# A delta rule in chunks of 64 tokens on quarter-array tiles, with 32-row blocks inverted on VectorE, instead of chunks of 128 inverted on TensorE

## The chip, the cores and the metric

One core of a Trainium2 chip runs the whole program. The metric is device time in microseconds of one launch; 1698.51 us is the median of three runs (1691.02 to 1699.28).

## The reference

Two blocks follow each other, all in float32. The first is a delta rule over 4 x 8 sequences (batch, head) of 768 tokens with 48 features. Each token reads its output and then updates a 48 x 48 state:

```
k_n = k / (norm(k) + 1e-6)
for t in range(S):
    y[t]  = q[t] @ state                 # the state before this token
    v_old = k_n[t] @ state
    state = state + beta[t] * outer(k_n[t], v[t] - v_old)
```

The outputs, 3072 tokens of 8 x 48 = 384 features, go to a router: cosine similarity to 8 expert embeddings over tau, softmax, and the first largest takes the token. The expert computes gate * relu(x @ w1[e]) @ w2[e] with 1024 hidden features.

## The kernel before

**Chunks.** A chunk is 128 tokens of one batch entry with its 8 heads; tokens lie on the partitions. With kb = beta k, a chunk needs z from (I + A) z = v - k S, where A is the strictly lower part of k kb^T; then y = q S + lower(q kb^T) z and S += kb^T z. There are 6 chunks a sequence and 4 batch entries.

**The functions.** `load` (L149) brings k, q and v of a chunk in pieces of 192 bytes, on SyncE's DMA queue. `prep` (L185 to L196) makes the norms, k over its norm and kb on GpSimd, heads padded to 64 columns. `front` transposes k, q and kb two heads at a time (L207, copied out at L208), multiplies them (L215) and masks the products (L220 on VectorE, L222 and L223 on ScalarE and GpSimd); L228 and L229 make the first W, the transposed inverses of the diagonal blocks of two rows.

**The inversion.** `invert` takes two batch entries at once, four groups of four heads. Six levels double the block from 2 to 128 rows. Each level transposes W (L240, copied at L242), multiplies by A (L248, masked at L251) and multiplies again (L257, added at L260), always whole 128 x 128 matrices, one head each.

**The steps.** `back` does what needs the state: k S (L268), R = v - k S (L271), z = W^T R (L276, copied at L279), q S (L284) plus the masked product times z (L287), the state's update (L299, L303), and the transposes and logits for the router (L307, L312, L313). `route` (L321 to L362) ranks each token within its expert, writes the outputs to DRAM (L343) and scatters token numbers into the experts' lists (L362).

**The experts.** 19 tiles of 256 tokens, each with one expert's weights. Per tile: gathered tokens are transposed (L447, L448), multiplied by w1 (L454, L456) and w2 (L460), scaled by the gate (L463) and scattered to the output (L464).

**What orders the work.** The code is written stage by stage, but a planner puts the instructions of each engine into a fixed order when the program is built: an instruction can be placed ahead of earlier code when its inputs and buffers are planned to be free. The engines then run their orders and wait on semaphores. PSUM's eight banks are shared out by two tags: `big` with five buffers, `seq` with three.

Of the kernel before, what the change touches and what calls it, by code (L numbers as in the profile page):

```python
# [15 lines left out]
C = 128  # tokens in a chunk of the delta rule  # L16
T = 256  # tokens in a tile of the experts
LEVELS = (2, 4, 8, 16, 32, 64)
# [3 lines left out]
def kernel(  # L22
# [30 lines left out]
    NMAP = E * N + NT * T  # L53

# [3 lines left out]
    idmap = tc.dram_tile([NMAP, 1], I32, name="idmap")  # L58

    def big(shape):  # L60
        return ps.tile(shape, F32, name="big", tag="big", bufs=5)

    def seq(shape):
        return ps.tile(shape, F32, name="seq", tag="seq", bufs=3)

# [5 lines left out]
    half = cpool.tile([128, B, H], F32, name="half")  # L71
    nc.vector.memset(half, 0.5)
    mask_su = cpool.tile([128, 1, 128], F32, name="mask_su")
    nc.gpsimd.memset(mask_su, 1.0)
    nc.gpsimd.affine_select(out=mask_su, in_=mask_su, compare_op=ALU.is_ge, fill=0.0, base=-1,
                            pattern=[[0, 1], [1, 128]], channel_multiplier=-1)
# [8 lines left out]
    tokid = cpool.tile([128, NC, B], I32, name="tokid")  # L85
    nc.gpsimd.iota(tokid, pattern=[[C, NC], [S, B]], base=0, channel_multiplier=1)
# [4 lines left out]
    nc.sync.dma_start(idmap.rearrange("(p n) o -> p (n o)", p=128), none)  # L91
    zrow = cpool.tile([1, Dm + 1], F32, name="zrow")
    nc.vector.memset(zrow, 0.0)
    nc.sync.dma_start(x_dram[N:N + 1, :], zrow)
# [5 lines left out]
    ac = att.enter_context(tc.tile_pool(name="ac", bufs=1))  # L100
    io = att.enter_context(tc.tile_pool(name="io", bufs=2))
# [3 lines left out]
    xor_i = ac.tile([128, 128], I32, name="xor_i")  # L105
    row_i = ac.tile([128, 128], I32, name="row_i")
    nc.gpsimd.iota(xor_i, pattern=[[1, 128]], base=0, channel_multiplier=0)
    nc.gpsimd.iota(row_i, pattern=[[0, 128]], base=0, channel_multiplier=1)
    nc.vector.tensor_tensor(xor_i, xor_i, row_i, op=ALU.bitwise_xor)
    xor_f = ac.tile([128, 128], F32, name="xor_f")  # L110
    nc.vector.tensor_copy(xor_f, xor_i)
    nmask1 = ac.tile([128, 1, 128], F32, name="nmask1")
    nc.vector.scalar_tensor_tensor(out=nmask1[:, 0, :], in0=xor_f, scalar=1.0, in1=mask_su[:, 0, :],
                                   op0=ALU.is_equal, op1=ALU.mult)
    nc.vector.tensor_scalar_mul(nmask1, nmask1, -1.0)
# [251 lines left out]
    for c in range(NC):  # L367
        V4 = loaded[1]
        if c + 1 < NC:
            loaded = load(c + 1)  # L370
# [133 lines left out]
```

## Time and profile before

| What | Value |
|---|---|
| Median of three runs | 1698.51 us |
| Span of the profiled execution (first to last instruction; no other time is given for it) | 1703.2 us |
| Instructions | 23067 |
| Mean granted TensorE clock | 0.864 of 2.4 GHz |
| Matmuls / busy | 9723 / 1476.8 us |
| VectorE, ScalarE, GpSimd busy | 568.2, 318.2, 350.3 us |
| DMA pieces, bytes | 114233, 92.62 MB |

The profile is one execution on the chip. PE is the matmul side of TensorE and PEld its weight loads, which overlap; DVE is VectorE, ACT ScalarE, POOL GpSimd, SP SyncE. A `q` behind an engine's name means its instruction queue, which issues DMAs. L12 is line 12 of the kernel. In a group, the shapes are output and input; a mean is the time of one instruction, which for matmuls includes time in the pipeline, so the spacing of a group on the timeline tells more of the pace.

### The profile page before, as it was taken

Reading aid. Unit: us, or ns where it says so; the run is one execution under the profiler, and the core shown is the slowest. Engines: PE = TensorE matmul, PEld = TensorE weight load, DVE = VectorE, ACT = ScalarE, POOL = GpSimd, SP = SyncE. Lnnn points to the kernel's source line nnn. Section 1 sums busy time; section 2 is a strip of 40 time slices with the busy share of each in tenths; the row PEclk is TensorE's granted clock in tenths of the full one; section 3 lists DMA queues with packets and bytes.
Section 4 is the critical chain, followed back from the end, with each engine's and each line's share of the span. In section 5 each row is a group of like instructions: output and inputs, shape, how many; then the busy total and the mean of one; then the engine's idle time right before and its main releaser. Section 6 shows DMA issues by size and latency. Waiting matters only on the chain. (4 is left out here: it accounts for less than half of the span.)

```text
span 1703.2 us, 23067 instructions
## 1 busy us (share of the span) xinstructions
PE 1476.8 (87%) x9723; PEld 1318.2 (77%) x9723; DVE 568.2 (33%) x1015; ACT 318.2 (19%) x613; POOL 350.3 (21%) x330
## 2 busy tenths in 40 slices
PE   3698969989698997989889897989739999999997
PEld 2697959979597996979789796979737666677774
DVE  4542525344362543526343352625401111001010
ACT  2122222121222212122212212222100000111110
POOL 7703042020503004030310204020021111111110
PEclk9786959789697977969788896979769999999999
DMA  9100030001200010000100000000045554555540
GB/s 144 19 1 10 1 65 1 6 5 20 47 1 10 1 43 6 1 10 1 38 1 1 1 1 19 2 1 1 19 171 184 173 180 159 163 179 178 165 145 0
DMA packets 114233, 92.62 MB, mean 54 GB/s; under 512 B 81137, under 2 KB 103849, under 8 KB 114130
## 3 DMA queue, kind: packets, MB, share of 16 engines
q1 hardware_dynamic: 108290, 78.80, 16.3%
q0 software_dynamic: 5632, 12.24, 2.6%
q8 instruction: 76, 1.25, 0.3%
q14 instruction: 27, 0.22, 0.0%
q10 hardware_dynamic: 208, 0.11, 0.0%
HBM read 81.55 MB, written 12.33 MB: 55 GB/s over the span
## 5 line engine op out<-in xcount | busy, mean ns | idle before, releaser
L251 DVE TENSOR_TENSOR Pm<-big,nmask 128x512 f32<-128x512 f32 x288 | 198.1, 691 | 308.8 <-PE big L248 308.8
L248 PE MATMUL big<-Ti,LM 128*128 128x128 f32 x2304 | 290.7, 288 | 0.0
L248 PEld LDWEIGHTS big<-Ti,LM 128*128 128x128 f32 x2304 | 285.9, 206 | 0.0
L257 PE MATMUL big<-W,Pm 128*128 128x128 f32 x2304 | 271.0, 276 | 9.1 <-DVE Pm L251 9.1
L257 PEld LDWEIGHTS big<-W,Pm 128*128 128x128 f32 x2304 | 264.8, 193 | 9.5 <-DVE Pm L251 9.5
L242 ACT ACTIVATE Ti<-big 128x512 f32<-128x512 f32 x288 | 152.7, 601 | 563.9 <-PE big L240 563.9
L240 PE MATMUL big<-ident,W 128*128 128x128 f32 x1152 | 157.8, 288 | 105.3 <-POOL W L229 105.3
L240 PEld LDWEIGHTS big<-ident,W 128*128 128x128 f32 x1152 | 134.8, 148 | 120.0 <-POOL W L229 116.7
L454 PE MATMUL big<-xTm,w 128*128 128x256 f32 x912 | 204.4, 384 | 18.4 <-DVE xTm L448 18.4
L260 DVE TENSOR_TENSOR W<-big,W 128x512 f32<-128x512 f32 x288 | 199.0, 691 | 57.6 <-PE big L257 57.5
L454 PEld LDWEIGHTS big<-xTm,w 128*128 128x128 f32 x912 | 173.5, 192 | 46.3 <-DVE xTm L448 23.0
L460 PE MATMUL seq<-w,hT 128*128 128x384 f32 x608 | 199.2, 486 | 0.0
L460 PEld LDWEIGHTS seq<-w,hT 128*128 128x128 f32 x608 | 115.5, 190 | 76.5
L463 DVE TENSOR_SCALAR y<-seq,xg 128x384 f32<-128x384 f32 x38 | 23.5, 618 | 390.5 <-PE seq L460 390.5
L196 POOL TENSOR_TENSOR KK<-KK,betaT 128x384 f32<-128x384 f32 x24 | 19.8, 830 | 600.4 <-PE seq L299 600.4
L456 ACT ACTIVATE hT<-big 128x512 f32<-128x512 f32 x76 | 45.4, 597 | 407.5 <-PE big L454 407.5
L464 POOL DMA_INDIRECT out_dram<-y,ids x38 | 38.3, 1008 | 239.5 <-DVE y L463 239.5
L215 PE MATMUL big<-KT 48*128 48x256 f32 x384 | 75.1, 511 | 10.0 <-ACT KT L208 10.0
L215 PEld LDWEIGHTS big<-KT 48*128 48x128 f32 x384 | 53.1, 248 | 22.0 <-ACT KT L208 14.8
L287 PE MATMUL seq<-Z,LM 128*128 128x48 f32 x384 | 66.4, 343 | 2.3 <-ACT Z L279 2.3
L287 PEld LDWEIGHTS seq<-Z,LM 128*128 128x128 f32 x384 | 65.2, 264 | 2.9 <-ACT Z L279 2.9
L436 POOL DMA_INDIRECT xg<-x_dram,ids x38 | 37.1, 977 | 130.6 <-DMA ids<-idmap 119.7
(131 smaller groups left out, 1076.9 us busy)
## 6 DMA issues: line engine op xcount, KB each, us to landing
w<-in_moe_w_dram SPq DMA_DIRECT2D x38, 1536.0 KB, 7.0
x_dram<-xc SPq DMA_DIRECT2D x6, 770.0 KB, 4.3
K<-in_k_dram SPq DMA_DIRECT2D x24, 192.0 KB, 4.1
V<-in_v_dram SPq DMA_DIRECT2D x24, 192.0 KB, 4.1
Qp<-in_q_dram SPq DMA_DIRECT2D x24, 192.0 KB, 2.9
xg<-x_dram,ids POOLq DMA_INDIRECT x38, 3.4
out_dram<-y,ids POOLq DMA_INDIRECT x38, 3.1
idmap<-tokid,slot_i POOLq DMA_INDIRECT x24, 4.1
```

The costliest lines, as they stand in the source:

```text
L215: nc.tensor.matmul(psG[:, i], lhsT=KT[pr, 2 * g + i, 2, :], rhs=KT[pr, 2 * g + i, 0:2, :], start=True, stop=True, skip_group_check=True)
L240: nc.tensor.transpose(psI[:, j, :], W[:, j, :], ident)
L242: nc.scalar.activation(Ti, psI, ACT.Copy)
L248: nc.tensor.matmul(psP[:, j, :], lhsT=AT[:, j, :], rhs=Ti[:, j, :], start=True, stop=True, skip_group_check=True)
L251: nc.vector.tensor_tensor(Pm, psP, nmask[s].broadcast_to([128, NP, 128]), op=ALU.mult)
L257: nc.tensor.matmul(psW[:, j, :], lhsT=Pm[:, j, :], rhs=W[:, j, :], start=True, stop=True, skip_group_check=True)
L260: nc.vector.tensor_tensor(Wn, psW, W, op=ALU.add)
L287: nc.tensor.matmul(psY[:, h, :], lhsT=LM[:, h % 2, h // 2, 1, :], rhs=Z[:, h, :], start=(c == 0 and h == 0), stop=True, skip_group_check=True)
L454: nc.tensor.matmul(psH[:, i, :], lhsT=w1[:, j, (f + i) * 128:(f + i + 1) * 128], rhs=xT[:, j, :], start=(j == 0), stop=(j == KC - 1))
L456: nc.scalar.activation(hT[:, f:f + 2, :], psH, ACT.Relu)
L460: nc.tensor.matmul(psO, lhsT=hT[:, f, t * 128:(t + 1) * 128], rhs=w2[:, f, :], start=(f == 0), stop=(f == NF - 1))
L464: nc.gpsimd.indirect_dma_start(out=out[:, :], out_offset=bass.IndirectOffsetOnAxis(ap=ids[:, t:t + 1], axis=0), in_=y, in_offset=None, bou ...
```

## The change

The chunk has 64 tokens, and two batch entries (g = 0, 1) are stacked on the partitions: tokens of the first on partitions 0 to 63, of the second on 64 to 127. With p the pair of entries, a superstep takes two chunks of both pairs, four tiles j; there are six supersteps. All products of the delta rule become matmuls on 64 x 64 tiles of the array (48 x 64 where the features are contracted), with the two halves written one after the other.

`front(s)` loads, normalizes, transposes k and q into KQ, multiplies k by k and q in one matmul per head and half (psG), and masks with beta folded into the mask (mb). `invert(s)` copies the 32 x 32 diagonal blocks of A through DRAM so that each of the 128 blocks (4 block rows by 32 heads) has one partition, inverts them there by forward substitution on VectorE (31 pairs of operations), copies the inverses back through DRAM, transposes them in blocks of 32 and makes the lower corner of each 64-row inverse with two products. `step` is the old `back` for a tile. The loop runs front and invert of superstep s + 1 ahead of the steps of s.

The sums of squares are taken tile by tile, k and q are loaded by half (24 transfers a superstep), and the outputs of a superstep are stored in four transfers instead of one per chunk. PSUM is shared out as `two` (three buffers of two banks) and `one` (two buffers of one bank), also in the experts. The constants for the old levels go. Initial transfers that don't belong to the loads move from SyncE's queue to ScalarE's.

```diff
-C = 128  # tokens in a chunk of the delta rule
-LEVELS = (2, 4, 8, 16, 32, 64)
+C = 64
+Q = 32
...
+    a_dram = tc.dram_tile([2, 4, J * H, Q, Q], F32, name="a_dram")
+    t_dram = tc.dram_tile([2, 4, J * H, Q, Q], F32, name="t_dram")
+    def two():
+        return ps.tile([128, 2, 512], F32, name="two", tag="two", bufs=3)
+    def one(shape):
+        return ps.tile(shape, F32, name="one", tag="one", bufs=2)
...
     def load(c):
+        Ks, Vs = [], []
+        for p in range(P2):
+            Kt = io.tile([128, H, D], F32, name="K", tag="K", bufs=4)
+            Vt = io.tile([128, H, D], F32, name="V", tag="V", bufs=8)
+            for dst, src in ((Kt, k), (Qs[(c * P2 + p) % len(Qs)][:, :, 0:D], q), (Vt, v)):
+                for g in range(2):
+                    nc.sync.dma_start(out=dst[64 * g:64 * g + 64],
+                                      in_=src[2 * p + g, :, c * C:(c + 1) * C, :].rearrange("h t d -> t h d"))
+            Ks.append(Kt)
+            Vs.append(Vt)
+        return Ks, Vs
+    def front(s):
+        data = [load(2 * s + i) for i in range(2)]
+        rn = wk.tile([128, J, H], F32, name="rn", tag="rn")
...
+        A = wk.tile([128, J, H, C], F32, name="A", tag="A")
+        kts, pts, kbs, vs = [], [], [], []
...
+            mb = wk.tile([128, 2, NP, C], F32, name="mb", tag="mb")
             for hh in range(2):
+                nc.gpsimd.tensor_tensor(mb[:, hh], later.broadcast_to([128, NP, C]),
+                                        bh.rearrange("p (a b) -> p b a", b=2)[:, hh].unsqueeze(2)
+                                        .broadcast_to([128, NP, C]), op=ALU.mult)
+            KQ = wk.tile([128, NP, 2, 2, C], F32, name="KQ", tag="KQ", bufs=8)
+            for i, src in enumerate((kn, qp)):
+                psT = one([128, NP, 2, C])
+                for hp in range(NP):
+                    nc.tensor.transpose(psT[:, hp].rearrange("p g t -> p (g t)"),
+                                        src[:, 2 * hp:2 * hp + 2, :].rearrange("p h d -> p (h d)"), ident)
+                nc.scalar.activation(KQ[:, :, :, i, :], psT, ACT.Copy)
+            psG = two()
+            for hp in range(NP):
+                for g in range(2):
+                    for hh in range(2):
+                        r = slice(64 * hh, 64 * hh + D)
+                        nc.tensor.matmul(psG[64 * g:64 * g + 64, hh, 128 * hp:128 * hp + 128],
+                                         lhsT=KQ[r, hp, g, 0, :], rhs=KQ[r, hp, g, :, :],
+                                         start=True, stop=True, skip_group_check=True)
+            pg = psG.rearrange("p a (b i t) -> p (a b) i t", i=2, t=C)
+            Pt = wk.tile([128, H, C], F32, name="P", tag="P", bufs=8)
+            mbf = mb.rearrange("p a b t -> p (a b) t")
+            nc.vector.tensor_tensor(A[:, j], pg[:, :, 0, :], mbf, op=ALU.mult)
+            nc.vector.tensor_tensor(Pt, pg[:, :, 1, :], mbf, op=ALU.mult)
...
+    def invert(s, A):
+        Bk = wk.tile([128, Q, Q], F32, name="Bk", tag="Bk", bufs=1)
+        for b in range(4):
+            nc.sync.dma_start(out=a_dram[s % 2, b].rearrange("h s t -> s h t"),
+                              in_=A[Q * b:Q * b + Q, :, :, Q * (b % 2):Q * (b % 2) + Q]
+                              .rearrange("s j h t -> s (j h) t"))
+        nc.sync.dma_start(out=Bk, in_=a_dram[s % 2].rearrange("b h s t -> (b h) s t"))
+        Tk = wk.tile([128, Q, Q], F32, name="Tk", tag="Tk", bufs=1)
+        nc.gpsimd.tensor_copy(Tk, eye)
+        for i in range(Q - 1):
+            sh = [128, Q - 1 - i, i + 1]
+            tmp = wk.tile([128, 256], F32, name="tmp", tag="tmp")
+            tv = tmp[:, 0:sh[1] * sh[2]].rearrange("p (a b) -> p a b", b=sh[2])
+            nc.vector.tensor_tensor(tv, Bk[:, i, i + 1:Q].unsqueeze(2).broadcast_to(sh),
+                                    Tk[:, i:i + 1, 0:i + 1].broadcast_to(sh), op=ALU.mult)
+            nc.vector.tensor_tensor(Tk[:, i + 1:Q, 0:i + 1], Tk[:, i + 1:Q, 0:i + 1], tv, op=ALU.subtract)
+        Td = wk.tile([128, J * H, Q], F32, name="Td", tag="Td", bufs=1)
+        nc.sync.dma_start(out=t_dram[s % 2].rearrange("b h s t -> (b h) s t"), in_=Tk)
+        for b in range(4):
+            nc.sync.dma_start(out=Td[Q * b:Q * b + Q], in_=t_dram[s % 2, b].rearrange("h s c -> s h c"))
+        Wd = wk.tile([128, J * H, Q], F32, name="Wd", tag="Wd", bufs=1)
+        nc.vector.transpose(Wd.rearrange("p h t -> p (h t)"), Td.rearrange("p h t -> p (h t)"))
+        Tz = wk.tile([128, J * H, Q], F32, name="Tz", tag="Tz", bufs=1)
+        nc.scalar.activation(Tz, Td, ACT.Copy, scale=first)
+        W = wk.tile([128, J * H, C], F32, name="W", tag="W")
+        nc.scalar.activation(W[:, :, 0:Q], Wd, ACT.Copy, scale=first)
+        for j in range(J):
+            psP = one([128, H, Q])
+            for h in range(H):
+                for g in range(2):
+                    r = slice(64 * g, 64 * g + 64)
+                    nc.tensor.matmul(psP[r, h, :], lhsT=A[r, j, h, :], rhs=Tz[r, j * H + h, :],
                                      start=True, stop=True, skip_group_check=True)
+            PI = PIs[j % len(PIs)]
+            nc.scalar.activation(PI[:, :, 0:Q], psP, ACT.Copy, scale=nsec)
+            psW = one([128, H, Q])
+            for h in range(H):
+                for g in range(2):
+                    r = slice(64 * g, 64 * g + 64)
+                    nc.tensor.matmul(psW[r, h, :], lhsT=PI[r, h, :], rhs=Wd[r, j * H + h, :],
                                      start=True, stop=True, skip_group_check=True)
+            nc.scalar.activation(W[:, j * H:(j + 1) * H, Q:C], psW, ACT.Copy)
+        return W
+    def step(s, j, KQ, Pt, kb, V, W, xc, ssx, lz):
+        c, p = 2 * s + j // P2, j % P2
+        Sp = St[p]
+        R = wk.tile([128, 2, NP, D], F32, name="R", tag="R")
+        Vv = V.rearrange("p (b a) d -> p a b d", a=2)
+        def heads(ps2):
+            return ps2[:, :, 0:NP * D].rearrange("p a (b d) -> p a b d", d=D)
+        psY = two()
+        yv = heads(psY)
         if c > 0:
+            psK = two()
+            kv = heads(psK)
+            for i, pv in ((0, kv), (1, yv)):
+                for hp in range(NP):
+                    for g in range(2):
+                        for hh in range(2):
+                            r = slice(64 * hh, 64 * hh + D)
+                            nc.tensor.matmul(pv[64 * g:64 * g + 64, hh, hp, :], lhsT=KQ[r, hp, g, i, :],
+                                             rhs=Sp[r, g, hp, :], start=(hp == 0), stop=True, skip_group_check=True)
+            nc.vector.tensor_tensor(R, Vv, kv, op=ALU.subtract)
+        else:
+            nc.vector.tensor_copy(R, Vv)
+        psZ = one([128, H, D])
+        Rf = R.rearrange("p a b d -> p (a b) d")
+        for h in range(H):
+            for g in range(2):
+                r = slice(64 * g, 64 * g + 64)
+                nc.tensor.matmul(psZ[r, h, :], lhsT=W[r, j * H + h, :], rhs=Rf[r, h, :],
                                  start=True, stop=True, skip_group_check=True)
         Z = wk.tile([128, H, D], F32, name="Z", tag="Z")
         nc.scalar.activation(Z, psZ, ACT.Copy)
+        if c < NC - 1:
+            psS = two()
+            sv = heads(psS)
+            for hp in range(NP):
+                for g in range(2):
+                    for hh in range(2):
+                        r = slice(64 * g, 64 * g + 64)
+                        nc.tensor.matmul(sv[64 * hh:64 * hh + 64, g, hp, :], lhsT=kb[r, 2 * hp + hh, :],
+                                         rhs=Z[r, hh * NP + hp, :], start=True, stop=True, skip_group_check=True)
+            nc.vector.tensor_tensor(Sp, Sp, sv, op=ALU.add)
+        for hp in range(NP):
+            for hh in range(2):
+                for g in range(2):
+                    r = slice(64 * g, 64 * g + 64)
+                    nc.tensor.matmul(yv[r, hh, hp, :], lhsT=Pt[r, hh * NP + hp, :], rhs=Z[r, hh * NP + hp, :],
+                                     start=(c == 0 and hp == 0), stop=True, skip_group_check=True)
+        xb = xc[:, j, 0:Dm]
+        nc.scalar.activation(xb.rearrange("p (b a d) -> p a b d", a=2, d=D), yv, ACT.Copy)
...
+    ahead = front(0)
+    W = invert(0, ahead[0])
+    for s in range(NS):
+        _, kts, pts, kbs, vs = ahead
+        xc = io.tile([128, J, Dm + 1], F32, name="xc", tag="xc")
+        ssx = wk.tile([128, J], F32, name="ssx", tag="ssx")
+        lz = wk.tile([128, J, E], F32, name="lz", tag="lz")
+        Wn = None
+        if s + 1 < NS:
+            ahead = front(s + 1)
+            Wn = invert(s + 1, ahead[0])
+        for j in range(J):
+            step(s, j, kts[j], pts[j], kbs[j], vs[j], W, xc, ssx, lz)
+        route(s, xc, ssx, lz)
+        W = Wn
...
-            psX = big([128, KC, 128])
+            psX = one([128, KC, 128])
...
-            psH = big([128, 2, T])
+            psH = two()
...
-            psO = seq([128, Dm])
+            psO = one([128, Dm])
```

## Rows read from the trace of the kernel before

**Rows 1.** The page: busy us, share of span, instructions by engine.
```profile
PE 1476.8 (87%) x9723; PEld 1318.2 (77%) x9723; DVE 568.2 (33%) x1015; ACT 318.2 (19%) x613; POOL 350.3 (21%) x330
```

**Rows 2.** Windows by stage: busy us (count) per engine, then clock, DMA share, GB/s.
```profile
50.00:1238.00 1188.00, 1045.24 (x8003) 1000.94 (x8002) 506.12 (x894) 262.57 (x520) 233.01 (x208) 0.82 0.05 12
1238.00:1276.00 38.00, 15.58 (x57) 12.61 (x58) 1.11 (x2) 2.39 (x4) 7.88 (x9) 0.61 0.52 187
1276.00:1703.00 427.00, 398.49 (x1578) 290.36 (x1576) 40.18 (x74) 43.00 (x72) 70.45 (x71) 0.99 0.48 153
```

**Rows 3.** Groups by line and shape: count, busy us, mean ns, idle before, TensorE.
```profile
L248 PE MATMUL big<-Ti,LM 128*128 128x128 f32 x2304 | 290.7, 288 | 0.0
...
L257 PE MATMUL big<-W,Pm 128*128 128x128 f32 x2304 | 271.0, 276 | 9.1 <-DVE Pm L251 9.1
...
L240 PE MATMUL big<-ident,W 128*128 128x128 f32 x1152 | 157.8, 288 | 105.3 <-POOL W L229 105.3
```

**Rows 4.** Timeline, one inversion level: start us, duration us, line, count.
```profile
287.83 3.74 PE L248 MATMUL big<-Ti,LM 128*128 128x128 f32 x32
...
296.72 3.74 PE L248 MATMUL big<-Ti,LM 128*128 128x128 f32 x32
```

**Rows 5.** Windows of ten us between two inversions: engines, then the granted clock.
```profile
215.00:225.00 10.00, 9.42 (x55) 9.08 (x55) 0.17 (x1) 1.45 (x4) 0.00 (x0) 0.50 0.46 79
```

**Rows 6.** Timeline, matmul groups outside the inversion, at both clock levels.
```profile
35.56 2.10 PE L215 MATMUL big<-KT 48*128 48x256 f32 x16 [0.69 <-ACT KT L208]
...
223.93 1.10 PE L299 MATMUL seq<-Z,KK 128*64 128x48 f32 x16
...
317.25 0.67 PE L299 MATMUL seq<-Z,KK 128*64 128x48 f32 x16
...
331.64 1.06 PE L207 MATMUL big<-ident,KK 128*128 128x128 f32 x4
```

**Rows 7.** Groups by line and shape, GpSimd and ScalarE.
```profile
L228 POOL TENSOR_TENSOR W<-LM,nmask 128x512 f32<-128x512 f32 x48 | 60.9, 1269 | 11.2 <-DVE LM L220 10.2
...
L196 POOL TENSOR_TENSOR KK<-KK,betaT 128x384 f32<-128x384 f32 x24 | 19.8, 830 | 600.4 <-PE seq L299 600.4
...
L279 ACT ACTIVATE Z<-seq 128x384 f32<-128x384 f32 x24 | 11.8, 491 | 168.5 <-PE seq L276 168.5
```

**Rows 8.** VectorE: two groups, then two dependent operations on the timeline.
```profile
L220 DVE TENSOR_TENSOR LM<-big,mask_su 128x512 f32<-128x512 f32 x48 | 33.2, 691 | 54.3 <-PE big L215 54.3
...
L271 DVE TENSOR_TENSOR R<-V,seq 128x384 f32<-128x384 f32 x20 | 11.1, 554 | 33.2 <-PE seq L268 33.2
...
234.67 0.17 DVE L354 TENSOR_TENSOR run<-run,rk 128x8 f32<-128x8 f32 x1
...
234.87 0.17 DVE L353 TENSOR_TENSOR rk<-rk,run 128x8 f32<-128x8 f32 x1
```

**Rows 9.** DMA: 10 to 30 us, 216 to 232 us, page's scatter.
```profile
q1 hardware_dynamic: 18002, 3.47, 119.3%
...
Qp<-in_q_dram SPq DMA_DIRECT2D x1, 192.0 KB, 2.8
...
idmap<-tokid,slot_i POOLq DMA_INDIRECT x24, 4.1
```

**Rows 10.** Timeline, order of instructions against the code.
```profile
14.36 0.21 POOL L392 IOTA thr_i<- 1x96 int32 x1
...
227.78 0.18 DVE L323 RECIPROCAL ssx<-ssx 128x4 f32<-128x4 f32 x1
...
228.04 0.17 DVE L313 COPY lz<-seq 128x8 f32<-128x8 f32 x1
```

**Rows 11.** Timeline, the first transposes of the delta rule.
```profile
24.66 1.12 PE L207 MATMUL big<-ident,KK 128*128 128x128 f32 x4 [6.35 <-POOL KK L194]
```

**Rows 12.** Timeline, change from one tile of the experts to the next.
```profile
1398.41 0.82 PE L447 MATMUL big<-ident,xg 128*128 128x128 f32 x6
...
1398.61 0.62 DVE L463 TENSOR_SCALAR y<-seq,xg 128x384 f32<-128x384 f32 x1 [4.54 <-PE seq L460]
```

More of the change, by code (lines that the diff above doesn't have):

```diff
@@ L176 @@
-    for j in range(KC):
-        nc.tensor.transpose(psE[:, j, :], esq[:, j * 128:(j + 1) * 128], ident[0:E, 0:E])
-    enT = ac.tile([128, KC, E], F32, name="enT")
-    nc.vector.tensor_copy(enT, psE)
-    def prep(c, K4):
-        Ksq = wk.tile([128, B, H, D], F32, name="Ksq", tag="Ksq", bufs=1)
-        nc.gpsimd.tensor_tensor(Ksq, K4, K4, op=ALU.mult)
-        rn = wk.tile([128, B, H], F32, name="rn", tag="rn")
-        nc.vector.tensor_reduce(rn, Ksq, axis=AX.X, op=ALU.add)
+    later = ac.tile([128, 1, C], F32, name="later")
@@ new lines @@
+    nc.vector.tensor_tensor(later[:, 0, :], mask_su[:, 0:C], mask_su[:, C:128], op=ALU.add)
+    nc.vector.tensor_scalar(later[0:C, 0, :], mask_su[0:C, 0:C], 1.0, None, op0=ALU.mult)
+    id2 = ac.tile([128, 1, Q], F32, name="id2")
+    nc.vector.tensor_tensor(id2[:, 0, :], ident[:, Q:2 * Q], ident[:, 3 * Q:4 * Q], op=ALU.add)
+    nsec = ac.tile([128, 1], F32, name="nsec")
+    nc.vector.tensor_reduce(nsec, id2, axis=AX.XY, op=ALU.add)
+    nc.vector.tensor_scalar_mul(nsec, nsec, -1.0)
+    first = ac.tile([128, 1], F32, name="first")
@@ new lines @@
+    nc.vector.tensor_scalar_add(first, nsec, 1.0)
+    eye = ac.tile([128, Q, Q], F32, name="eye")
+    nc.gpsimd.memset(eye, 0.0)
+    nc.gpsimd.affine_select(out=eye, in_=eye, compare_op=ALU.not_equal, fill=1.0, base=0,
+                            pattern=[[1, Q], [-1, Q]], channel_multiplier=0)
+    Qs, KNs, KBs, PIs = [], [], [], []
+    for i in range(4):
+        Qs.append(ac.tile([128, H, 64], F32, name=f"Qp{i}"))
+        nc.gpsimd.memset(Qs[i], 0.0)
+    for i in range(4):
+        KNs.append(ac.tile([128, H, 64], F32, name=f"KN{i}"))
+        nc.vector.memset(KNs[i], 0.0)
@@ L263, in back @@
-    def back(c, b, kk, KT, LM, Ws, V, xc, ssx, lz):
-        if c > 0:
-            psK = seq([128, H, D])
-            for j in range(NP):
-                nc.tensor.matmul(psK[:, 2 * j:2 * j + 2, :], lhsT=KT[:, j, 0, :], rhs=S_bd[:, b, j],
-                                 start=True, stop=True, skip_group_check=True)
-            R = wk.tile([128, H, D], F32, name="R", tag="R")
-            nc.vector.tensor_tensor(R, V, psK, op=ALU.subtract)
-        else:
-            R = V
-        psZ = seq([128, H, D])
-        for h in range(H):
-            nc.tensor.matmul(psZ[:, h, :], lhsT=Ws[h % 2][:, h // 2, :], rhs=R[:, h, :],
-                             start=True, stop=True, skip_group_check=True)
+        A = wk.tile([128, J, H, C], F32, name="A", tag="A")
@@ L305, in back @@
[L305 to L307 removed]
+        if c < NC - 1:
+            psS = two()
+            sv = heads(psS)
+            for hp in range(NP):
+                for g in range(2):
+                    for hh in range(2):
[3 more added lines that the diff above has]
+            nc.vector.tensor_tensor(Sp, Sp, sv, op=ALU.add)
@@ L308, in back @@
+        nc.scalar.activation(ysq, xb, ACT.Square, accum_out=ssx[:, j:j + 1])
+        psX = one([128, KC, 128])
+        for i in range(KC):
+            nc.tensor.transpose(psX[:, i, :], xb[:, i * 128:(i + 1) * 128], ident)
         xT = wk.tile([128, KC, 128], F32, name="xT", tag="xT")
         nc.scalar.activation(xT, psX, ACT.Copy)
-        psL = seq([128, E])
-        for j in range(KC):
-            nc.tensor.matmul(psL, lhsT=xT[:, j, :], rhs=enT[:, j, :], start=(j == 0), stop=(j == KC - 1))
@@ L313, in back, with route @@
-        nc.vector.tensor_copy(lz[:, b, :], psL)
-    def route(c, xc, ssx, lz):
+        psL = one([128, E])
+        for i in range(KC):
+            nc.tensor.matmul(psL, lhsT=xT[:, i, :], rhs=enT[:, i, :], start=(i == 0), stop=(i == KC - 1))
+        nc.vector.tensor_copy(lz[:, j, :], psL)
+    def route(s, xc, ssx, lz):
         def t(name, shape):
             return wk.tile(shape, F32, name=name, tag=name)
-        be = [128, B, E]
+        be = [128, J, E]
         nc.gpsimd.tensor_tensor(out=ssx, in0=ssx, in1=half[:, :, 0], op=ALU.pow)
@@ L362, in route @@
             nc.gpsimd.indirect_dma_start(
[L363 to L384 removed]
+                out=idmap[:, :], out_offset=bass.IndirectOffsetOnAxis(ap=slot_i[:, j:j + 1], axis=0),
@@ L444, in experts @@
         for t in range(2):
-            psX = big([128, KC, 128])
+            psX = one([128, KC, 128])
             for j in range(KC):
```

282 lines of the change are left out of this document (87 added, 195 removed).

## The prediction, made before the changed kernel ran

> **What bounds the kernel now.** I read the engines' busy times first [rows 1]: TensorE is at work for 87% of the span, VectorE for a third. The stretches [rows 2] then split that: the delta rule runs to about 1238 us and the experts take the rest, 465 us. Both keep TensorE busy, but the change rewrites only the first, so the experts' stretch enters the sum nearly as it is. In the first stretch the groups by line [rows 3] show who fills TensorE: 2304 matmuls on L248, as many on L257 and 1152 transposes on L240, so 5760 of 8003 matmuls belong to the doubling that inverts the 128-row blocks. The timeline [rows 4] shows its beat: the same group starts again 8.89 us later, six times per pair of sequences, with TensorE packed. Outside these levels (transposes, products, state) the granted clock falls to 0.50, the 1.2 GHz level [rows 5], and the same matmuls take longer: 16 of 64 columns take 0.67 us at the upper level and 1.10 us at the lower [rows 6]. So the stage is bound by the amount of TensorE work, most of it the inversion.
>
> **What the change removes.** The six levels: per chunk two pairs, per pair six times 8.9 us, so 12 x 6 x 8.9 = 641 us of the stage's 1188 us in [rows 2], with their evictions on VectorE and ScalarE. The masks and the first W, 2 x 1.27 us on GpSimd per half [rows 7], go too. I can't subtract this and stop, because the rest is rewritten as well; I build the new stage from below. A superstep is two chunks of all four sequences, four tiles (j = 0 to 3) of 2 x 64 tokens; there are six.
>
> **TensorE per superstep.** Matmuls on 64x64 tiles: front 4 x 16, the two products of invert 4 x 32, steps 4 x 80 (K 16, Y 16, Z 16, S 16, P 16): 512. The nearest row is L299 (64 columns of weights, 48 streamed, two column halves in turn): 42 ns each at full clock, 69 ns at half [rows 6]. At half clock 512 x 69 = 35.3 us. The 32 full transposes of front, the 12 of the outputs and the 12 logit matmuls I take at the 1.06/4 = 0.265 us of a full transpose at half clock [rows 6], 14.8 us. Sum 50 us at half clock, about 30 at full. Below is no row for four tiles at once, which could be cheaper; above, no overlap of tiles at all, at most the 0.265 us that a whole 128x128 pass takes at half clock.
>
> **VectorE per superstep.** The forward substitution is 31 pairs of operations on (31-i)(i+1) elements, 5456 in all, twice. Small dependent operations follow each other every 0.20 us at 8 elements (L354 at 234.67, L353 at 234.87), and the slope between 384 and 512 elements is (691-554)/128 = 1.07 ns an element [rows 8]: 62 x 0.20 + (10912 - 496) x 1.07 ns = 23.5 us. No row has the short broadcast runs of this chain (inner runs of 1 to 31); from below, only the elements count, 10912 x 1.07 ns = 12 us; from above I allow each operation the 0.55 us of a 384-element one, 34 us. Beside it A and P 8 x 0.69 = 5.5, the sums of squares 4 x 0.55, R and state 8 x 0.55 = 4.4 (L220 and L271 in [rows 8]), the block transpose about 1.1, routing some 30 x 0.20 = 6: 43 us in all. So neither engine fills more than about 50 us.
>
> **GpSimd.** Per tile two products at 0.83 us and two masks of 256 columns at half of the 1.27 us of 512 [rows 7]: 2.9 us, 12 us per front.
>
> **DMA.** At full use 18002 pieces went in 20 us, 1.11 ns each over all engines; one load of 1024 pieces landed after 2.8 us, so about 1.7 us are fixed [rows 9]. A superstep loads 12288 pieces as before (13.6 us, in twice as many transfers). The inversion adds two transfers of 4096 pieces of 128 B, 4.6 + 1.7 = 6.3 us each, and two contiguous ones of 512 KB, at 187 GB/s [rows 2] 2.8 + 1.7 = 4.5 each. Storing pieces of 128 B to DRAM has no row. From below they go by bytes, 3 us; from above like the 4-byte scatter, 128 of them landing in 4.1 us [rows 9], which would be absurdly long for 4096 (131 us), but is kept as a rival. I take 6.3, by the row with the nearest piece size.
>
> The Trainium skill, page DMA: Bandwidth & Descriptors, section Specifications, says that below 512 B a transfer loses line rate because the engine reads and writes back. By it the 4096-piece store would take about twice its 4.6 us, an estimate from that page and the row together; the 192 B loads reach 174 GB/s, so reads here don't show it, and no run here stores such pieces. It would add about 5 us to a latency, some 12 us to the whole.
>
> **How the parts stand in time.** Is the new order serial? The planner takes instructions out of program order when they are ready: the constant of L392, which the code makes after the whole delta rule, ran at 14.4 us, and the routing operation L323 ran ahead of the copy L313 of the step before it [rows 10]. So I let the steps of superstep s run inside the transfers and the substitution of s+1, as the code's order asks. Buffers close the loop: KQ, P and kb have 8 buffers, four a superstep, so front(s+2) waits for steps(s). The loop over two supersteps is:
> - tail of front, by GpSimd: 12 us;
> - inversion: 6.3 (A out) + 4.5 (blocks in) + 23.5 and some 8 of other VectorE work between + 4.5 + 6.3 (inverse out and in) + 2.5 for the copies + about 10 for four tiles of two products (16 x 69 ns = 1.1 us, a copy, and waits of 0.2) = 66; the loads of the next superstep stand once in the same queues, 13.6: 79 us;
> - steps: a chain K 1.1, R 0.55, Z 1.1, copy 0.49 [rows 7], S 1.1, state 0.55 with waits, 5.8 us; but TensorE needs 80 x 69 ns + 6 x 0.265 = 7.1 us for a step, and its order is fixed, so 4 x 10 = 40 us.
> Together 131 us for two, 65.5 for one. Because TensorE at half clock is taken 50 of these, I take 72 us a superstep. Fully serial, with front 26 and routing 8, it would be 140.
>
> **The sum.** In the old trace the first transposes start at 24.7 us [rows 11]; the new start needs K of two chunks, so 29, then 12 + 2.5 for front and 57 for an undisturbed inversion: 100 us. Then five supersteps of 72, 360. The last steps have nothing beside them, 40, with some 40 small operations of routing at 0.20 and its waits, 10: 50. The experts: 465 [rows 2]. There psX and psO now share two PSUM buffers. In the old trace the transposes L447 of both halves run at once from 1398.4, beside the eviction L463 at 1398.6 [rows 12]; now the second half waits for that eviction (0.62 us and a wait), about 0.4 us a tile, 7 us over 18 tiles. If the planner finds no better order it could be 1 us, 18; if it was hidden, 0. Sum 100 + 360 + 50 + 472 = 982 us of span, against 1703.2 now. The span read here lies 4.7 us above the median of the timed runs, 1698.5, and the profile gives no other time for that execution; so I forecast 978 us.
>
> **Rivals.**
> - *Serial supersteps*: the inversion has higher priority and stands ahead of the steps in TensorE's or SyncE's fixed order, and a transfer that takes longer than planned stops everything. For it: SyncE's queue is one line of 24 loads, 10 inversion transfers and 4 stores per superstep, any of which can wait. Against it: [rows 10]. 140 us: 100 + 700 + 50 + 472 - 5 = 1317 us.
> - *TensorE becomes the bound again*: the two row halves of psP, psW and psZ lie in one PSUM bank. If such pairs don't overlap, 192 matmuls a superstep cost at most the 0.265 us of a full pass instead of 0.069, 38 us more, 88 us of TensorE work, and with waits 95 us a superstep: 100 + 475 + 50 + 472 - 5 = 1092 us. The rows show two row halves overlapping (L215: 16 matmuls of 256 columns in 2.10 us at full clock [rows 6]) but into different banks.
> The Trainium skill, page TensorEngine Tiling (Array Packing), section Restrictions and Gotchas, states just that: different row tiles can't access the same PSUM bank at once. No row here has both halves in one bank.
> - *Slower*: the 128 B transfers. If 8192 pieces per inversion cost over 20 ns each instead of 1.11, they take 164 us, the loop can't hide them, and a superstep needs 219 us: 100 + 1095 + 50 + 472 - 5 = 1712 us, slower than now; that is the point from which it decides, and at the scatter's 4.1 us for 128 it would be far past it. Against it: every piece-wise transfer in the trace runs at a twentieth of that.
> - *Better overlap*: no queueing and TensorE often at full clock, 53 us a superstep: 882 us.
>
> **Chances.** The forecast (58 to 90 us a superstep, 908 to 1067 us) 0.62; TensorE-bound 0.17; serial or nearly so 0.12; better 0.05; slower 0.03; no change 0.01. Range 890 to 1200 us, which holds the forecast, the TensorE-bound case and a part of the serial one (up to 116 us a superstep). What a measurement here can tell from no change is about 0.5%, 8 us. Faster 0.96, same 0.01, slower 0.03.
>
> **What the new profile would show.** The substitution's operations at a mean near 0.38 us, 31 pairs in 23 to 32 us, six times; the A store landing in about 6 us; TensorE's granted clock near 0.5 to 0.7 in the first half and its busy share well below 87%; 64-wide matmuls near 69 ns apart; an expert stretch of 465 to 485 us. Wrong would be: steps that start only after the inversion of the next superstep has ended (serial), Z, P and W products at several times the pace of the K and S ones (bank), or transfers of tens of microseconds.

## The result and the profile after

The changed kernel took 1251.07 us, median of runs from 1248.66 to 1252.12, beside 1694.76 us for the kernel before on the same chip: a ratio of 0.738 [0.736, 0.740]. It is much faster, but 273 us later than the forecast and above the range. The profiled execution took 1248.6 us of span, so its marks can be set against the sum of 982 us. In the experiments below one run of e5, slower at a lower granted clock (1234.44 us), is left out of its figure.

From the page of the kernel after: busy time, share of the span and instructions of the engines, then TensorE's busy share and granted clock over 40 slices of 31 us.

```profile
PE 781.4 (63%) x8033; PEld 632.4 (51%) x8033; DVE 304.9 (24%) x821; ACT 160.7 (13%) x313; POOL 240.6 (19%) x259
...
PE   0306128801980088209813985299999999999996
...
PEclk9755555655555555655565555599999999999998
```

TensorE, at work for 87% of the span before [rows 1], now has six holes in the first 25 slices, one per superstep, and from the third of these slices on the granted clock lies near 0.5, the 1.2 GHz level. The stretches show how much falls to which stage (busy us and count of PE, weight loads, DVE, ACT and POOL, then clock, DMA share, GB/s; the fourth is one hole):

```profile
50.00:778.00 728.00, 352.40 (x6224) 320.32 (x6224) 242.84 (x690) 108.84 (x226) 130.78 (x131) 0.54 0.20 39
778.00:816.00 38.00, 13.71 (x55) 11.61 (x56) 1.12 (x2) 1.89 (x4) 7.69 (x8) 0.62 0.53 187
816.00:1248.00 432.00, 402.99 (x1580) 290.42 (x1578) 41.88 (x74) 43.49 (x73) 70.67 (x71) 0.99 0.47 151
257.00:307.00 50.00, 0.00 (x0) 0.00 (x0) 25.63 (x69) 0.58 (x1) 12.49 (x11) 0.50 0.27 57
```

The delta rule ends at 778 us against 1238 before [rows 2]. The experts took 432 us against 427, as forecast. TensorE did not start one instruction in the hole from 257 to 307 us. The waits name its end (engine, line, tile waited for: us in all, times, longest):

```profile
PE one L285 <- ACT Tz L277: 313.5, 6, 58.4
```

```profile
ACT Tz L277 <- DMA Td<-t_dram: 324.8, 6, 61.4
```

TensorE waits 313.5 us for the inverse to come back from DRAM. The timeline of that superstep shows what it leaves undone meanwhile (start, duration, line, tile out<-in, count, idle time before):

```profile
254.81 2.24 SPq L257 DMA_DIRECT2D a_dram<-A  x4
255.29 0.55 DVE L321 TENSOR_TENSOR R<-V,two 128x384 f32<-128x384 f32 x1
...
262.54 0.34 SPq L260 DMA_DIRECT2D Bk<-a_dram  x1
...
266.38 0.19 DVE L267 TENSOR_TENSOR tmp<-Bk,Tk 128x31 f32<-128x31 f32 x1 [10.55 <-DMA Bk<-a_dram]
...
298.72 0.34 SPq L271 DMA_DIRECT2D t_dram<-Tk  x1
...
301.38 2.21 SPq L273 DMA_DIRECT2D Td<-t_dram  x4
...
306.42 1.15 ACT L277 ACTIVATE Tz<-Td,first 128x1024 f32<-128x1024 f32 x1 [60.04 <-DMA Td<-t_dram]
307.62 1.92 PE L285 MATMUL one<-Tz,A 64*64 64x32 f32 x32 [57.67 <-ACT Tz L277]
...
322.84 1.92 PE L293 MATMUL one<-Wd,PI 64*64 64x32 f32 x32 [0.63 <-ACT PI L288]
324.56 1.92 PE L329 MATMUL one<-R,W 64*64 64x48 f32 x32
327.08 1.10 PE L341 MATMUL two<-Z,KB 64*64 64x48 f32 x32 [0.59 <-ACT Z L332]
```

The key product K of the previous superstep's first step is done, and R = V - K is ready at 255.84. Its Z (L329) needs nothing of the running inversion, yet it starts at 324.56, behind all eight products L285 and L293 of it. In the code the psP, psW and psZ tiles all carry the tag `one`, with two PSUM buffers. TensorE's order in the trace has the products of all four tiles first: L285 and L293 in turn, four times over, and only then L329, L341 and L348.

### The profile page after: what moved, and what is told of

Same layout as the page of the kernel before. It is cut to its first block, busy times and chain, and to the rows that moved or that the text cites. A ratio compares the mean times of both kernels' runs of the same rounds, so it can differ in the third digit from the quotient of the medians.

```text
span 1248.6 us, 18748 instructions
## 1 busy us (share of the span) xinstructions
PE 781.4 (63%) x8033; PEld 632.4 (51%) x8033; DVE 304.9 (24%) x821; ACT 160.7 (13%) x313; POOL 240.6 (19%) x259
## 5 line engine op out<-in xcount | busy, mean ns | idle before, releaser
L285 PE MATMUL one<-Tz,A 64*64 64x32 f32 x768 | 45.7, 291 | 313.5 <-ACT Tz L277 313.5
L503 PE MATMUL two<-xTm,w 128*128 128x256 f32 x912 | 203.4, 383 | 12.3 <-DVE xTm L497 12.3
L285 PEld LDWEIGHTS one<-Tz,A 64*64 64x64 f32 x768 | 43.7, 222 | 314.6 <-ACT Tz L277 314.6
L509 PE MATMUL one<-w,hT 128*128 128x384 f32 x608 | 199.2, 486 | 0.0
L503 PEld LDWEIGHTS two<-xTm,w 128*128 128x128 f32 x912 | 172.8, 191 | 40.0 <-DVE xTm L497 17.0
L509 PEld LDWEIGHTS one<-w,hT 128*128 128x128 f32 x608 | 115.5, 190 | 76.5
L512 DVE TENSOR_SCALAR y<-one,xg 128x384 f32<-128x384 f32 x38 | 23.5, 618 | 389.5 <-PE one L509 389.5
L267 DVE TENSOR_TENSOR tmp<-Bk,Tk 128x31 f32<-128x31 f32 (+15 forms) x186 | 71.1, 382 | 52.5 <-DMA Bk<-a_dram 46.6
L269 DVE TENSOR_TENSOR Tk<-Tk,tmp 128x31 f32<-128x31 f32 (+15 forms) x186 | 68.2, 367 | 5.9
L319 PE MATMUL two<-S,KQ 48*64 48x48 f32 x1408 | 56.8, 294 | 6.5 <-DVE P L246 6.5
L293 PE MATMUL one<-Wd,PI 64*64 64x32 f32 x768 | 46.1, 292 | 14.6 <-ACT PI L288 14.6
L319 PEld LDWEIGHTS two<-S,KQ 48*64 48x64 f32 x1408 | 47.6, 202 | 13.2 <-issue 12.2
L293 PEld LDWEIGHTS one<-Wd,PI 64*64 64x64 f32 x768 | 42.8, 220 | 17.8 <-ACT PI L288 17.8
L329 PE MATMUL one<-R,W 64*64 64x48 f32 x768 | 49.2, 303 | 0.0
L329 PEld LDWEIGHTS one<-R,W 64*64 64x64 f32 x768 | 47.0, 223 | 0.1
L348 PE MATMUL two<-Z,P 64*64 64x48 f32 x768 | 46.3, 303 | 0.7 <-ACT Z L332 0.6
```

The costliest lines, as they stand in the source:

```text
L267: nc.vector.tensor_tensor(tv, Bk[:, i, i + 1:Q].unsqueeze(2).broadcast_to(sh), Tk[:, i:i + 1, 0:i + 1].broadcast_to(sh), op=ALU.mult)
L269: nc.vector.tensor_tensor(Tk[:, i + 1:Q, 0:i + 1], Tk[:, i + 1:Q, 0:i + 1], tv, op=ALU.subtract)
L285: nc.tensor.matmul(psP[r, h, :], lhsT=A[r, j, h, :], rhs=Tz[r, j * H + h, :], start=True, stop=True, skip_group_check=True)
L293: nc.tensor.matmul(psW[r, h, :], lhsT=PI[r, h, :], rhs=Wd[r, j * H + h, :], start=True, stop=True, skip_group_check=True)
L319: nc.tensor.matmul(pv[64 * g:64 * g + 64, hh, hp, :], lhsT=KQ[r, hp, g, i, :], rhs=Sp[r, g, hp, :], start=(hp == 0), stop=True, skip_group ...
L329: nc.tensor.matmul(psZ[r, h, :], lhsT=W[r, j * H + h, :], rhs=Rf[r, h, :], start=True, stop=True, skip_group_check=True)
```

## Experiments

Theory A: this order makes the supersteps serial, because the tiles of one tag are given out in the order of the code, in which the next inversion stands ahead of the steps. Rival B: TensorE's work itself, slowed by row halves that share a PSUM bank. Rival C: the substitution and the transfers are the path whatever the order.

**e1: no lookahead.** Front, inversion, steps and routing of a superstep, one after another, in the code.

```diff
-    ahead = front(0)
-    W = invert(0, ahead[0])
     for s in range(NS):
...
+        A, kts, pts, kbs, vs = front(s)
+        W = invert(s, A)
...
```

> The loop is written without lookahead: front and inversion of a superstep stand right before its own steps. Theory A (in the changed kernel the lookahead hides almost nothing, because the steps wait behind the next inversion's products): about the same, 1251 to 1275 us; only the first superstep's overlap is lost. Rival B (the lookahead already hides most of the steps, and the time goes elsewhere): the 40 us of steps come out into the open in five supersteps, 1251 + 200 = about 1450 us.

Measured: 1256.21 us, ratio 0.741 [0.738, 0.744], against 0.738 [0.736, 0.740]. The Tz copies stand 124 us apart (100.59, the sixth at 720.79). In the kernel after those from the second to the sixth also stand 124 us apart (177.69 to 673.92), and only the first interval is shorter, 78 us:

```profile
99.57 1.15 ACT L277 ACTIVATE Tz<-Td,first 128x1024 f32<-128x1024 f32 x1 [54.30 <-DMA Td<-t_dram]
...
177.69 1.15 ACT L277 ACTIVATE Tz<-Td,first 128x1024 f32<-128x1024 f32 x1 [49.87 <-DMA Td<-t_dram]
```

No steps stand in it, because those of the first superstep come behind the second inversion; they are paid at the end, where the steps of two supersteps follow the last inversion instead of one. So the lookahead gains nothing per superstep and, as the two ratios overlap, at most some 5 us in all. That is what A expects.

**e2: a tag of their own for the inversion's products.** The PSUM space is the same, `one` gives up a buffer.

```diff
-        return ps.tile(shape, F32, name="one", tag="one", bufs=2)
+        return ps.tile(shape, F32, name="one", tag="one", bufs=1)
+    def inv(shape):
+        return ps.tile(shape, F32, name="inv", tag="inv", bufs=1)
...
-            psP = one([128, H, Q])
+            psP = inv([128, H, Q])
...
-            psW = one([128, H, Q])
+            psW = inv([128, H, Q])
```

> The inversion's products get a PSUM tag of their own with one buffer, and the tag called one keeps one buffer; code order and bank count stay. Theory A (the steps' Z has to take its PSUM buffer behind the next inversion's products, in the order of the code, since both use one tag): Z moves ahead of those products, the steps run while VectorE substitutes, the period of 124 us falls by up to the 40 us of steps, to about 85: near 1050 us, somewhat more since single buffers make each copy wait. Rival B (the planner's own times put the products first): no change in order, 1251 or slower through the single buffers. Rival C (transfers and substitution are the limit whatever the order): above 1200.

Measured: 1144.0 us, 0.675 [0.672, 0.677]. The wait shrinks from 313.5 to 42.6 us, and Z now stands between the products of the inversion (waits, then timeline of TensorE):

```profile
PE inv L288 <- ACT Tz L280: 42.6, 3, 21.2
```

```profile
386.15 1.92 PE L288 MATMUL inv<-Tz,A 64*64 64x32 f32 x32 [0.48 <-ACT W L298]
387.88 1.28 PE L332 MATMUL one<-R,W 64*64 64x48 f32 x20
```

The delta rule ends at 611.0 us instead of 777.6, so A holds: nothing but the tags and their buffers changed, and the order changed with them, so it was not the planner's own times that put the products first. The pace of the products did not change, L288 takes the 1.92 us of L285. The gain is 167 us there; the experts give back 62, since their transposes and output products now share one buffer:

```profile
708.54 5.43 PE L512 MATMUL one<-w,hT 128*128 128x384 f32 x16 [0.71 <-DVE y L515]
...
714.68 0.55 PE L499 MATMUL one<-ident,xg 128*128 128x128 f32 x3 [0.71 <-DVE y L515]
```

Both wait for y, the eviction of the buffer that they share.

**e3: products behind the steps, tags as after.** invert ends at Td; what follows it (Wd, Tz, W, the products) becomes `finish`, called behind the four steps.

```diff
+        return Td
+    def finish(s, A, Td):
         Wd = wk.tile(...)
...
-            Wn = invert(s + 1, ahead[0])
+            Tn = invert(s + 1, ahead[0])
         (the four steps)
+        if s + 1 < NS:
+            Wn = finish(s + 1, ahead[0], Tn)
```

> The inversion is cut in two in the code: transfers and substitution of the next superstep stand ahead of the steps, its two products behind them. PSUM as in the changed kernel. Theory A (order of buffers): as with an own tag but with two buffers, 1020 to 1080 us, substitution spread out by the steps' operations on VectorE, TensorE idle for under 20 us a superstep instead of 52. Rival B (planner's times): the same gain, since the code's order is moved too. Rival C (transfers and substitution are the limit): above 1200.

Measured: 1170.26 us, 0.691 [0.688, 0.694], 90 us above the upper end of what A expected (waits, then TensorE's timeline):

```profile
PE one L288 <- ACT Tz L280: 216.5, 6, 54.5
```

```profile
331.44 1.92 PE L296 MATMUL one<-Wd,PI 64*64 64x32 f32 x32 [0.63 <-ACT PI L291]
...
334.16 1.09 PE L231 MATMUL one<-ident,KN 128*128 128x128 f32 x4
...
395.44 1.45 PE L365 MATMUL one<-enT,xT 128*128 128x8 f32 x6 [0.58 <-ACT xT L362]
431.97 1.92 PE L288 MATMUL one<-Tz,A 64*64 64x32 f32 x32 [35.09 <-ACT Tz L280]
```

Code order counts, but it takes only a third of the wait away. In the new order the transposes of the next front (L231, of the tag `one` too) stand behind the last product of the inversion. So the next inversion starts late and has only the four steps beside it; they end at 396.9, and TensorE waits 35 us. In e7 below, with the tag apart, these transposes run ahead of the products (L234 at 337.32, Tz only at 361.41). That the tag alone holds them back in e3 is not shown.

**e4: two banks.** The row halves of psP and psW lie in two banks. For this the two tiles move from the tag `one` to the tag `two`, and each half has a copy of its own (a single run).

```diff
-            psP = one([128, H, Q])
+            psPt = two()
+            psP = psPt[:, :, 0:H * Q].rearrange("p g (h t) -> p g h t", t=Q)
...
-                    nc.tensor.matmul(psP[r, h, :], ...
+                    nc.tensor.matmul(psP[r, g, h, :], ...
```

> The two row halves of the inversion's products go to two PSUM banks, with a copy for each half. Read from the spacing of the products, not from the time, since the buffers' order changes too. Theory bank (row halves in one bank don't overlap): 32 passes take about 1.1 us, as those of the state's update do, instead of 1.92. Theory tiles (only two of the four array tiles are used by these products, so each is used again at every second pass): 1.9 us as before.

Measured: 1241.32 us, from which nothing is read. The trace shows each float32 matmul of the code as two instructions (a transpose as one); I call one a pass. 26 passes with the halves in two banks took 1.65 us, 63 ns each:

```profile
298.51 1.65 PE L297 MATMUL two<-Wd,PI 64*64 64x32 f32 x26
```

In one bank 32 took 1.92, 60 ns (L285 above). So the bank is not what slows them: B falls as a matter of banks, and an engine that waits 313.5 us for the inverse is not bound by its own work. The products that use two array tiles (the diagonal ones: L285, L293, L329, L348) take 60 ns a pass, those that use four in turn (L341) 1.10/32 = 34 ns, at the same clock. A group's duration holds some time in the pipeline as well (a single pass shows as 0.29 us). From start to start of groups back to back it is 1.72/32 = 54 ns (L293 at 310.12, L285 at 311.84) and 0.88/32 = 27 ns (L341 at 327.08, L348 at 327.96): twice as long with half the tiles. This fits the theory of tiles in the expectation, but no run changed the tiles alone.

The tag moved something too. The first step's K and Y products take tag `two`; in the kernel after they run ahead of the hole, in e4 behind it:

```profile
247.36 0.63 PE L319 MATMUL two<-S,KQ 48*64 48x48 f32 x32
```

```profile
308.19 1.77 PE L325 MATMUL two<-S,KQ 48*64 48x48 f32 x48
```

The superstep stays at 124 us (second Tz at 164.15, sixth at 660.48). So a tag shared with the steps keeps them behind the inversion also when it is the other tag, as A says.

**e5: half of the substitution, order as after.** 15 of the 31 pairs of operations, which leaves the rest of the inverse out.

```diff
-        for i in range(Q - 1):
+        for i in range((Q - 1) // 2):
```

> The changed kernel with only the first 15 of the 31 pairs of the substitution, so the inverses are left incomplete. Theory A (the steps wait for the next inversion, so every microsecond of the substitution lies open): 15 of the 31 pairs take about half of the 27 us, so about 13.5 us less in each of six supersteps, 81 us: near 1170. Rival (the substitution is hidden behind the steps): no change, 1251.

Measured: 1171.0 us, 0.691 [0.687, 0.694]: 80 us less. TensorE's wait falls by 78, from 313.5 to 235.3 us:

```profile
PE one L285 <- ACT Tz L277: 235.3, 6, 46.4
```

In the order of the kernel after the substitution lies on the path in full. A and C both expect this.

**e6: e2, and PSUM of their own for the experts.** The delta rule's pool is closed ahead of them; five buffers take psX and psH, three take psO.

```diff
+    ps2 = ctx.enter_context(tc.tile_pool(name="ps2", ...))
...
-            psX = one([128, KC, 128])
+            psX = big([128, KC, 128])
...
-            psO = one([128, Dm])
+            psO = seq([128, Dm])
```

> As e2, and the experts get PSUM buffers of their own as in the kernel before (five and three) once the delta rule has ended. Theory (e2's experts lost 53 us, from 476 to 529 after the delta rule, because their one buffer for transposes and outputs is emptied before TensorE goes on): 1144 - 60 = about 1084, the experts' stretch back at 465. Rival (the experts' loss came from elsewhere): 1144.

Measured: 1078.7 us, 0.636 [0.633, 0.639]. The delta rule ends at 610.4 us, as in e2; the 65 us are the experts' alone.

**e7: e6 with two buffers for each tag.**

```diff
-        ... name="two", tag="two", bufs=3)
+        ... name="two", tag="two", bufs=2)
-        ... name="one", tag="one", bufs=1)
+        ... name="one", tag="one", bufs=2)
-        ... name="inv", tag="inv", bufs=1)
+        ... name="inv", tag="inv", bufs=2)
```

> As e6, but the eight banks are dealt as two buffers of two banks, two for the steps and fronts, two for the inversion's products (e6: three, one, one). If single buffers hold up the transposes and the products in e6, faster: 1040 to 1070. If the third buffer of two banks matters more (outputs, k S and the state's update are held at once in a step): slower than e6, above 1090.

Measured: 1057.15 us, 0.623 [0.620, 0.626]. The delta rule ends at 589.6 us. Its timeline shows the steps running inside the substitution, which is what the forecast had counted on:

```profile
230.22 0.36 DVE L270 TENSOR_TENSOR tmp<-Bk,Tk 128x192 f32<-128x192 f32 x1
230.23 0.49 ACT L335 ACTIVATE Z<-one 128x384 f32<-128x384 f32 x1 [4.22 <-PE one L332]
230.77 0.94 PEld L344 LDWEIGHTS two<-Z,KB 64*64 64x64 f32 x32 [0.74 <-ACT Z L335]
230.77 1.11 PE L344 MATMUL two<-Z,KB 64*64 64x48 f32 x32 [0.58 <-ACT Z L335]
...
231.94 0.55 DVE L346 TENSOR_TENSOR S<-S,two 128x384 f32<-128x384 f32 x1 [1.36 <-PE two L344]
...
232.41 0.61 DVE L272 TENSOR_TENSOR Tk<-Tk,tmp 128x192 f32<-128x192 f32 x1
```

The state update (L344, L346) of superstep s stands between two operations (L270, L272) of the substitution of s+1. TensorE's waits in e7:

```profile
PE inv L288 <- ACT Tz L280: 66.7, 6, 22.0
...
PE one L405 <- DVE xc L395: 23.2, 5, 6.1
```

**e8 and e11: half of the substitution, in e6 and in e7; e10: e7 without the products P Z in eleven of the twelve chunks.** They ask what is still on the path. e8 and e11 leave out what e5 does; the edit of e10 is

```diff
-        for hp in range(NP):
+        for hp in range(NP if c == 0 else 0):
```

> e6 with only the first 15 of the 31 pairs of the substitution, so the inverses are left incomplete. If the substitution is still on the path in e6, near 81 us less than e6. If TensorE's work and the steps' chain set the pace there, as the prediction assumed for the changed kernel: under 30 us less.

> e7 with only the first 15 of 31 pairs of the substitution (inverses left incomplete). In e7 TensorE waits 67 us in all for the inverse, of which the first superstep's are most of what can't be hidden. If the inversion's latency still sets the pace: 60 to 80 us less, near 985. If TensorE does: 15 to 30 less, from the first superstep and the last waits.

> e7 without the products of P and Z in ten of the twelve chunks (their part of the outputs is left out): 20 of 24 tiles lose 32 passes of 60 ns, 1.9 us each, and the wait behind them. If TensorE's amount of work sets the pace in e7: 20 x 1.9 = 38 us less, near 1019. If the inversion's latency sets it: under 12 us less.

Measured: e8 1066.62 us, 0.629 [0.627, 0.632], 12 us below e6. e11 1014.58, 0.597 [0.594, 0.601], 43 below e7, between what the two theories expected. e10 1021.19, 0.602 [0.599, 0.605], 36 below e7. Here `c` counts the chunks, so all but the first lose the product, eleven of twelve and not the ten of the expectation: 64 of 768 passes are left, and TensorE as the only bound would have given 22 x 1.92 = 42. With one buffer (e6) the substitution is nearly free; what sets the pace there is not shown. With two (e7) both count in part, so neither theory holds alone. C, by which the substitution and the transfers are the path whatever the order, is wrong: what e5 shows is true of the order of the kernel after.

**e9: e7 with the routing of a superstep later**, behind the next front and inversion in the code. The L405 row above showed TensorE held by it.

```diff
+        if s > 0:
+            route(*pend)
         for j in range(J):
             step(s, j, ...)
-        route(s, xc, ssx, lz)
+        pend = (s, xc, ssx, lz)
...
+    route(*pend)
```

> e7, with the routing of a superstep put in the code behind the next front and inversion. In e7 TensorE stands 6 us a superstep before the routing's two products, with the next front behind them in its order. If that wait lies on the loop: up to 6 x 6 = 36 us less than e7's 1057, near 1025. If the wait on the inversion (8.5 us a superstep) only grows by as much: 1050 to 1060.

Measured: 1037.38 us, 0.612 [0.609, 0.615], between the two times expected and the fastest version that computes everything; the delta rule ends at 570.7 us. The wait for Tz stays:

```profile
PE inv L288 <- ACT Tz L280: 69.0, 6, 17.1
```

## Why the prediction was wrong

I set the forecast's marks beside those of the kernel after. An inversion's products end 18.3 us after Tz starts (306.42 to 324.76), so the first ended at about 118 us and the last at 673.92 + 18.3 = 692. Of the five intervals between the Tz copies the first has no steps in it (e1).

| term | forecast, us | measured, us |
|---|---|---|
| to the end of the first inversion | 100 | 118 |
| five supersteps | 5 x 72 = 360 | 78 + 4 x 124 = 574 |
| last steps and routing | 50, of one superstep | 777.6 - 692 = 85, of two |
| experts | 472 | 471 |
| sum | 982 | 1248 |

**The failed step** is in "How the parts stand in time": "So I let the steps of superstep s run inside the transfers and the substitution of s+1, as the code's order asks." [rows 10] showed instructions of other engines moved ahead when their operands were ready, and I took that for TensorE's products as well. I listed the buffers in SBUF that close the loop and left out the PSUM tags, though I had used just such a shared tag for the experts. e1 shows that the order gained next to nothing over a serial one, e2 that the tag was the reason: with it apart, superstep and tail alike shrink (delta rule 778 to 611 us). My serial rival named the right outcome at 140 us a superstep and gave it 0.12, but for other reasons (a priority, a slow transfer) than the tag; serial cost 124.

The first inversion adds 18 us: its transposes start at 34.8 instead of 29, its products take 18 instead of 12.5, and its substitution was not undisturbed: it took 36.5 us (55.95 to 92.46), in which VectorE waited 5.3 us for GpSimd's part of the next front, and ten operations took some 0.93 us each instead of 0.4 while GpSimd was at work (70.69 to 80.20).

**The second miss** is the 50 us of TensorE work. By its terms it is 65 in the kernel after. The groups (busy us, mean ns, then idle time before) show why:

```profile
L285 PE MATMUL one<-Tz,A 64*64 64x32 f32 x768 | 45.7, 291 | 313.5 <-ACT Tz L277 313.5
...
L329 PE MATMUL one<-R,W 64*64 64x48 f32 x768 | 49.2, 303 | 0.0
...
L341 PE MATMUL two<-Z,KB 64*64 64x48 f32 x704 | 24.3, 307 | 13.0 <-ACT Z L332 13.0
```

L329 is 16 matmuls a step in the code and 32 passes in the trace (768 over 24 steps). The rows that I priced with count passes, 16 of L299 [rows 6] for 8 matmuls of the code, while my 512 counted matmuls of the code. Four tiles at once halve the pass from 69 to 34 ns and would have made that good, but the diagonal products take 60. The seven groups of 64-row products are busy 297 us, 49.6 a superstep against 35.3; transposes and logits 15.8 against 14.8. In the kernel after this miss lies on the path only where the 18 us of products per superstep (8 x 1.7 and waits, against 10) and the tail show it; in e7, where the order is mended and 36 of the 42 us of such work lay on the path (e10), it helps to hold a superstep at 84.5 us (first Tz at 106.53, sixth at 529.14), not at 72.

**What was right.** The substitution:

```profile
L267 DVE TENSOR_TENSOR tmp<-Bk,Tk 128x31 f32<-128x31 f32 (+15 forms) x186 | 71.1, 382 | 52.5 <-DMA Bk<-a_dram 46.6
...
L269 DVE TENSOR_TENSOR Tk<-Tk,tmp 128x31 f32<-128x31 f32 (+15 forms) x186 | 68.2, 367 | 5.9
```

139.3/6 = 23.2 us against 23.5, and 32.3 with what stands between (266.38 to 298.69) against 31.5. The second agreement is luck in part: the forecast's 8 us were other VectorE work, but 5.4 of the 9.1 measured are VectorE waiting for one GpSimd operation on 128 x 32 elements:

```profile
DVE rn L209 <- POOL rn L208: 32.5, 6, 5.6
```

The four transfers: A out and stored 7.7 us (6.3), blocks in 3.8 (4.5), inverse out 2.7 (4.5), in 5.0 (6.3), in all 19.2 against 21.6. Their issues (KB each, median us to landing):

```profile
a_dram<-A SPq DMA_DIRECT2D x24, 128.0 KB, 2.8
...
Td<-t_dram SPq DMA_DIRECT2D x24, 128.0 KB, 2.7
```

The slower rival needed tens of microseconds here and is out. These stores of 1024 pieces landed in 2.8 us, as long as the load of 1024 pieces that the forecast went by [rows 9]. The Trainium skill (DMA: Bandwidth & Descriptors, section Specifications) says that below 512 B the engine reads, modifies and writes back. No doubling by it shows at this size. The bank rival failed as a price: e4 moved the row halves to two banks without a faster pass. The Trainium skill (TensorEngine Tiling (Array Packing), section Restrictions and Gotchas) says that different row tiles can't use one bank at the same time. No price of that shows in e4.

**What stays open.** The forecast's order, with the tags apart, ends the delta rule at 590 us (e7) or 571 (e9), and the sum had it at 510. Extra TensorE work and the substitution each hold a part (e10, e11). The trace of e7 shows how they come to add up: the blocks are asked for at 283.13, and such a load lands in 3.7 us, but VectorE begins the substitution only at 306.01, behind the state updates of the first two steps, which wait for TensorE:

```profile
283.13 0.35 SPq L263 DMA_DIRECT2D Bk<-a_dram  x1
...
295.92 0.56 DVE L346 TENSOR_TENSOR S<-S,two 128x384 f32<-128x384 f32 x1 [17.82 <-PE two L344]
...
305.54 0.55 DVE L346 TENSOR_TENSOR S<-S,two 128x384 f32<-128x384 f32 x1 [4.07 <-PE two L344]
306.01 0.18 DVE L270 TENSOR_TENSOR tmp<-Bk,Tk 128x31 f32<-128x31 f32 x1
```

In four of the six supersteps the substitution starts 23 to 35 us after its load was issued. No run changed this order, so how much of the 80 us it holds is open.

## What to carry to other kernels

Before counting on overlap, list which tiles share a PSUM tag and in which order the code asks for them: a tile that is ready early and one that is ready late should not share one, and here a tag of its own was worth 167 us of the delta rule, and PSUM apart for the two stages 65 more. Price products in passes as the trace counts them, by the number of array tiles that take turns. When a stage that was packed becomes a chain, ask of every link what may run inside it, and look for the empty stretch in the windows first.

## What the runs showed of the hardware

At the 1.2 GHz level a 64x64 float32 pass took 34 ns with four array tiles in turn and 60 with two (27 and 54 from start to start), whether those two wrote one PSUM bank or two. An operation of the substitution on 128 x 252 elements took VectorE 0.93 us while GpSimd was at work (72.78, first inversion of the kernel after) and 0.42 us when it was not (80.51). The granted clock of a record can contradict the matmuls themselves: in e2 the delta rule's window shows 1.00 (the figure behind the five engines), while L288 takes the same 1.92 us for 32 passes as L285 does at 0.50. And 32 passes of K there take 1.05 us, against 0.63 in the kernel after (L319 under e4) in a window from 240 to 250 us that shows 0.99.

```profile
375.13 1.05 PE L322 MATMUL two<-S,KQ 48*64 48x48 f32 x32
```

```profile
50.00:611.00 561.00, 390.27 (x6296) 346.49 (x6288) 234.07 (x695) 110.55 (x228) 134.40 (x135) 1.00 0.24 51
```
